# Two weight chunks per 256-token step, and a new order of the pieces, in a recurrence with two MLP layers

## The chip, the cores and the metric

One core of one Trainium2 chip runs the whole program. The metric is device time in microseconds; the median of three runs is compared.

## The reference

A gated linear recurrence over 768 time steps, for 4 batches and 8 heads of 48 channels, and then two MLP layers on all 3072 tokens, each 384 -> 2048 -> 384 wide:

```python
for t in range(S):
    state = alpha[:, :, t, :, None] * state + einsum('bhd,bhe->bhde', k[:, :, t], v[:, :, t])
    y[:, :, t] = einsum('bhd,bhde->bhe', q[:, :, t], state)
x = y.transpose(0, 2, 1, 3).reshape(3072, 384)
h = x @ w_in;   x = (h * tanh(softplus(h))) @ w_out      # layer 0
h = x @ w2_in;  out = (h * cos(h)) @ w2_out              # layer 1
```

The weights arrive as 64-bit floats.

## The kernel before

**Recurrence.** The 768 steps are cut into 12 chunks of 64; with two halves of the batch-heads (`hb`) that makes 24 units, in the list `order`. A unit loads decays (`ld_a`), keys, queries and values; two running products on VectorE (`scan`, L290, and `scan2`, L308) turn decays into factors; `keys` (L312) and `queries` (L322) multiply them in; TensorE does `turn` (L339), `scores` (L353, L354), `out_mm` (L370, L371) and `state_mm` (L431); `causal` (L360, L361) masks. The state is carried in the tiles `three` and scaled by GpSimd (`state_mul`, L450). `QPOOL` and `KPOOL` list the units whose `queries` and `keys` run on GpSimd instead of VectorE. The first eight units (`n < 8`) have start times of their own (`EARLY`); later ones are tied to MLP steps.

**Blocks and steps.** Tokens form 6 blocks of 512 (two chunks of 64 time steps x 4 batches), weights 16 chunks (`fc`) of 128 hidden channels. A step is one block and one weight chunk: nine matmuls into the PSUM tile `h` (`mm1`, L484 to L486), an elementwise chain, nine matmuls into three accumulators `acc` (`mm2`, L544 to L546). Both products are done with a high and a low part of each operand, three matmuls per product. In layer 0 the chain is sigmoid, arctan (`angle`, L492, L493) and sine (`sines`, L497) on ScalarE, a product (`gated`, L500) and the rounded high part (`act_c`, L524, a cast on VectorE; in layer 1 the cast is L526 on ScalarE), and the low part (`pool_c`, L531) on GpSimd. Sigmoid and arctan need one activation table, sine another, so sines are done for two steps at a time (`PAIR`, `pairs`). In layer 1 the chain is L505, L509, L512, L515, L518.

The first five chunks of block 0 run as half steps of 256 tokens (`HALVES`): all five on the first 256 tokens (`c0 = 0`), for which units 0 and 1 are enough, then all five on the second 256. `SHARED` makes two neighbouring blocks go through the same chunks one after the other: block 0 with chunks 0 to 7, block 1 with 0 to 7, then 8 to 15 for each.

**Weights.** A chunk is loaded (`ld_w`, L205) and converted: `conv_a` (L214, VectorE) moves low bits; the sign is taken either by `conv_a2` (L218, VectorE) or, for the chunks in `SIGNS`, by `conv_s` (L223, ScalarE); `conv_b` (L228, ScalarE) rescales, `conv_c` (L232, VectorE) joins, `conv_d` rounds the high part (L238 on ScalarE, or L236 on VectorE for chunks in `ROUNDS`), `conv_e` (L241, GpSimd) gives the low part. Layer 1's chunks are converted while layer 0 ends, in the tiles `three`. At most five raw chunks (tag `x`) are there at once.

**The order.** Every instruction is a piece with an engine, a cost, a due time, predecessors and buffers. `Plan.order` plays the pieces through once with these costs: whenever an engine is free it starts the ready piece with the smallest due time whose buffers are free. Instructions are emitted in that order, and each engine then runs its own instructions in it. All loads go through SyncE's queue. The due times are made of constants: `START`, `STEP`, `EARLY`, `CONV` (how long ahead of its first use a chunk is converted), `LOAD_K` and the like.

Of the kernel before, what the change touches and what calls it, by code (L numbers as in the profile page):

```python
# [13 lines left out]
F32 = mybir.dt.float32  # L14
# [22 lines left out]
START = [2.41] * 5 + [1.14] * 5 + [0.29] * 6  # L37
ATT = -0.89
# [4 lines left out]
BASE = (-1.08, 1.07, 2.87, 9)  # L43
LAG = 0.27
LOAD_K, LOAD_Q, LOAD_V, LOAD_W = 0.34, 0.74, 3.21, 9.99
LATE = -8.64
SPLIT = 7.29, 2.05
CONV = (5.15,) * 4 + (8.17,) * 4 + (30.0,) * 8
ELEM, SECOND, EVAC, FILLED = 7.7, 5.39, 5.39, -1.58
# [92 lines left out]
def chunked_path(ctx: ExitStack, tc: tile.TileContext, q, k, alpha, v1, ve, vo, w1, w2, const, out):  # L142
# [5 lines left out]
    def stile(shape, dtype, tag, name):  # L148
        return sb.tile(shape, dtype, tag=tag, bufs=BUFS[tag], name=name)
# [315 lines left out]
    for la, b, f0, f1 in phases:  # L465
        nh = HALVES.get((la, b), 0) if f0 == 0 else 0
        starts[len(steps)] = (la, b, f0)
        steps += [(la, b, fc, c, c + UT) for c in (0, UT) for fc in range(nh)] + [(la, b, fc, 0, N) for fc in range(max(nh, f0), f1)]
        ends[len(steps) - 1] = (la, b, f0)
        if f1 < NFC:  # L470
            split.add((la, b))
    phase_of = {}
# [4 lines left out]
    def mm1(i):  # L477
        la, b, fc, c0, c1 = steps[i]
        h = h_[i] = ps.tile([P, c1 - c0], F32, tag="h", bufs=3, name="h")
        hi, lo = wh[la, fc], wl[la, fc]  # L480
        for kc in range(3):
            f = slice(kc * P, kc * P + P)
            xh, xl = (x[:, kc, c0:c1] for x in xr[la, b])
            nc.tensor.matmul(h, hi[:, f], xh, start=kc == 0, stop=False)  # L484
            nc.tensor.matmul(h, hi[:, f], xl, start=False, stop=False)  # L485
            nc.tensor.matmul(h, lo[:, f], xh, start=False, stop=kc == 2)  # L486
# [3 lines left out]
    def angle(i):  # L490
        ta_[i] = stile([P, steps[i][4] - steps[i][3]], F32, "ta", "ta")
        nc.scalar.activation(ta_[i], h_[i], AF.Sigmoid, scale=-1.0)  # L492
        nc.scalar.activation(ta_[i], ta_[i], AF.Arctan)  # L493
# [26 lines left out]
    def act_c(i):  # L520
        la, b, fc, c0, c1 = steps[i]
        gh_[i] = stile([P, c1 - c0], F32R, "gh", "gh")
        if la == 0:
            nc.vector.tensor_copy(gh_[i], ta_[i])  # L524
        else:
            nc.scalar.copy(gh_[i], ta_[i])  # L526

    def pool_c(i):
        la, b, fc, c0, c1 = steps[i]
        gl_[i] = stile([P, c1 - c0], F32R, "gl", "gl")  # L530
        nc.gpsimd.tensor_tensor(gl_[i], ta_.pop(i), gh_[i].bitcast(F32)[:, :], op=ALU.subtract)  # L531

    def mm2(i):
        la, b, fc, c0, c1 = steps[i]
# [4 lines left out]
        hi, lo = wh[la, fc], wl[la, fc]  # L539
        gh, gl = gh_.pop(i), gl_.pop(i)  # L540
        first, last = i in starts, i in ends
        for d in range(3):
            f = slice(DM + d * P, DM + d * P + P)
            nc.tensor.matmul(acc[d][:, c0:c1], hi[:, f], gh, start=first, stop=False, skip_group_check=True)  # L544
            nc.tensor.matmul(acc[d][:, c0:c1], lo[:, f], gh, start=False, stop=False, skip_group_check=True)  # L545
            nc.tensor.matmul(acc[d][:, c0:c1], hi[:, f], gl, start=False, stop=last, skip_group_check=True)  # L546
# [30 lines left out]

    ticks = {}
# [14 lines left out]
    def dve(alone, beside):  # L593

        return lambda now: (beside if plan.free[POOL] > now + 0.3 * alone else alone, LAG)

    def dma(kib):
        return lambda now: (kib / 330.0, 2.0)

    due = [T0]  # L600
    for i, st in enumerate(steps):
        due.append(due[-1] + (STEP if st[4] - st[3] == N else HSTEP) + (START[i] if i < len(START) else ATT if st[0] == 0 and st[1] < NB - 1 else 0.0))
    n0 = sum(st[0] == 0 for st in steps)

    pairs, i = [], 0
    while i < n0:
        left = next(e for e in ends if e >= i) + 1 - i
        size = left % PAIR if i in starts and left % PAIR else PAIR
        pairs.append(list(range(i, i + size)))
        i += size  # L610
# [16 lines left out]
    for i, (la, b, fc, c0, c1) in enumerate(steps):  # L627
        half = c1 - c0 < N
        w = (lambda x: 0.5 * x + 0.05) if half else (lambda x: x)
# [25 lines left out]
        add(("act_c", i), DVE if la == 0 else ACT, dve(w(0.42), w(0.75)) if la == 0 else w(0.57), d + (6.2 if la == 0 else 7.3) - ELEM, functools.partial(act_c, i), [(prev, i), ("act_c", i - 1)], [("gh", ("gh", i))], [])  # L655
        add(("pool_c", i), POOL, w(1.4), d + 8 - ELEM, functools.partial(pool_c, i), [("act_c", i), ("pool_c", i - 1)], [("gl", ("gl", i))], [("ta", i)])
        add(("mm2", i), PE, pe(w(2.04)), d2, functools.partial(mm2, i), [("pool_c", i)] + ([("mm2", i - 1)] if i else []),
            [(f"acc{x}", ("acc", *phase_of[i], x)) for x in range(3)] if i in starts else [], [("gh", i), ("gl", i)] + [("w", la, fc), ("w2", la, fc)])
# [67 lines left out]
    index = {ph: i for i, ph in starts.items()}  # L726
    at_step = {2: index[0, 0, SHARED[0, 0]], 3: index[0, 2, 0] - 4, 4: index[0, 3, 0] - 8, 5: index[0, 4, 0] - 12}
    beside = {b: due[i] for b, i in at_step.items()}
    gate = {2: index[0, 1, 0] + 2, **{b: at_step[b] - 1 for b in range(3, NB)}}
    for n, s in enumerate(order):  # L730
# [20 lines left out]
        add(("keep_end", s), POOL, 0.6, d + 1, f(keep_end, s), [("scan", s)], [], [("Pt", n)])  # L751
# [224 lines left out]
```

## Time and profile before

| | |
|---|---|
| median of three runs | 958.46 us (958.07 to 958.48) |
| the profiled execution | 957.87 us, of which the span from first to last instruction is 956.1 us |
| TensorE busy | 908.7 us, 95% |
| ScalarE busy | 705.6 us, 74% |
| VectorE busy | 564.1 us, 59% |
| GpSimd busy | 471.0 us, 49% |
| mean granted TensorE clock | 0.988 |

Busy shares are means over stages that differ: the start, where TensorE lacks work, and long stretches in which it never stops. A table by stretch is of more use.

### The profile page before, as it was taken

How to read it: one execution, taken by the hardware profiler on the slowest of the kernel's cores; microseconds unless marked ns; L12 is line 12 of the kernel's file. 1: busy time of each engine (PE TensorE's matmuls, PEld its weight loads, DVE VectorE, ACT ScalarE, POOL GpSimd, SP SyncE). 2: the span in 40 equal slices, each digit the busy share in tenths (PEclk: the TensorE clock that was granted, in tenths of full speed). 3: DMA queues.
4: the chain of work that ended last, by engine and by line, in shares of the span. 5: the costliest groups of instructions: out<-in, count | busy, mean ns of one | idle time of the engine just before them, and what ended most of it. 6: DMA issues, size and time to landing. Idle time of an engine off the chain costs nothing.

```text
span 956.1 us, 15552 instructions
## 1 busy us (share of the span) xinstructions
PE 908.7 (95%) x5972; PEld 741.2 (78%) x5972; DVE 564.1 (59%) x757; ACT 705.6 (74%) x1077; POOL 471.0 (49%) x344
## 2 busy tenths in 40 slices
PE   5688889999999999999999999999999999999997
PEld 4577667788877787888887768788888888888886
DVE  7588999848847757612699697534443423333331
ACT  4999599777678688687999899866655666655653
POOL 4756748636336445343378567534423424332333
PEclk9979899999999999999999999999999999999999
DMA  8542543212313312120022222000000000000000
GB/s 252 172 131 90 171 129 110 68 34 75 92 44 99 91 44 85 38 72 1 27 80 93 70 95 99 2 1 1 34 34 1 1 33 1 34 1 1 34 0 36
DMA packets 25183, 59.09 MB, mean 62 GB/s; under 512 B 3856, under 2 KB 7568, under 8 KB 25104
## 3 DMA queue, kind: packets, MB, share of 16 engines
q1 hardware_dynamic: 25104, 58.05, 19.0%
q8 instruction: 47, 0.77, 0.3%
q14 instruction: 32, 0.26, 0.1%
HBM read 52.53 MB, written 4.72 MB: 60 GB/s over the span
## 4 chain that ended last, share of the span: by engine, by line
PE 71%; DVE 11%; ACT 8%; issue 4%; DMA 3%; POOL 2%; SPq 0%; POOLq 0%; DVEq 0%; ACTq 0%
PE acc L544 11%; PE h L484 11%; PE acc L546 11%; PE acc L545 11%; PE h L486 11%; PE h L485 11%; PE sc L353 2%; PE y L370 2%; DVE three L214 1%; DVE three L232 1%; PE dS L431 1%; DVE ta L500 1%; DVE three L218 1%; POOL three L322 1%; ACT three L223 1%
## 5 line engine op out<-in xcount | busy, mean ns | idle before, releaser
L531 POOL TENSOR_TENSOR gl<-ta,gh 128x512 fp32r<-128x512 f32 (+1 forms) x197 | 288.6, 1471 | 341.6 <-ACT gh L526 202.0
L484 PE MATMUL h<-xhi,wh 128*128 128x512 f32 (+1 forms) x591 | 234.0, 396 | 7.9 <-DVE ta L500 4.8
L544 PE MATMUL acc<-gh,wh 128*128 128x512 f32 (+1 forms) x591 | 232.0, 393 | 0.0
L546 PE MATMUL acc<-gl,wh 128*128 128x512 f32 (+1 forms) x591 | 228.5, 387 | 2.8 <-POOL gl L531 2.8
L486 PE MATMUL h<-xhi,wl 128*128 128x512 f32 (+1 forms) x591 | 229.0, 387 | 0.8 <-POOL wl L241 0.8
L485 PE MATMUL h<-xlo,wh 128*128 128x512 f32 (+1 forms) x591 | 229.2, 388 | 0.0
L545 PE MATMUL acc<-gh,wl 128*128 128x512 f32 (+1 forms) x591 | 227.4, 385 | 0.0
L512 DVE SCALAR_TENSOR_TENSOR tb<-tb,ta 128x512 f32<-128x512 f32 x96 | 80.5, 838 | 116.6 <-ACT tb L509 116.6
L484 PEld LDWEIGHTS h<-xhi,wh 128*128 128x128 f32 x591 | 112.6, 191 | 36.3 <-DVE ta L500 8.0
L546 PEld LDWEIGHTS acc<-gl,wh 128*128 128x128 f32 x591 | 111.4, 188 | 27.0 <-POOL gl L531 4.8
L486 PEld LDWEIGHTS h<-xhi,wl 128*128 128x128 f32 x591 | 112.9, 191 | 23.8 <-POOL wl L241 1.3
L544 PEld LDWEIGHTS acc<-gh,wh 128*128 128x128 f32 x591 | 111.2, 188 | 23.5 <-issue 0.6
L485 PEld LDWEIGHTS h<-xlo,wh 128*128 128x128 f32 x591 | 112.9, 191 | 21.0
L545 PEld LDWEIGHTS acc<-gh,wl 128*128 128x128 f32 x591 | 111.4, 188 | 21.1
L518 DVE TENSOR_TENSOR ta<-h,tb 128x512 f32<-128x512 f32 x96 | 66.4, 692 | 94.3 <-ACT tb L515 94.3
L500 DVE TENSOR_TENSOR ta<-h,ta 128x512 f32<-128x512 f32 (+1 forms) x101 | 65.5, 662 | 74.5 <-ACT ta L497 73.5
L505 ACT ACTIVATE ta<-h 128x512 f32<-128x512 f32 x96 | 57.4, 598 | 68.8 <-POOL gl L531 42.0
L526 ACT CAST gh<-ta 128x512 fp32r<-128x512 f32 x96 | 59.9, 624 | 48.3 <-PE acc L545 45.8
L492 ACT ACTIVATE ta<-h 128x512 f32<-128x512 f32 (+1 forms) x101 | 58.2, 577 | 35.7 <-PE h L486 33.8
L492 ACT ACT_TABLE_LOAD x50 | 64.2, 1283 | 25.6 <-PE h L486 24.7
L450 POOL TENSOR_TENSOR three<-three,aend 48x384 f32<-48x384 f32 x44 | 43.9, 997 | 47.7 <-DVE three L443 41.5
L497 ACT ACT_TABLE_LOAD x51 | 65.4, 1283 | 0.9
(119 smaller groups left out, 1262.9 us busy)
## 6 DMA issues: line engine op xcount, KB each, us to landing
wr<-in_w_dram SPq DMA_DIRECT2D x16, 768.0 KB, 5.4
three<-in_w_dram SPq DMA_DIRECT2D x16, 768.0 KB, 4.2
at<-in_alpha_chunks_dram SPq DMA_DIRECT2D x23, 227.9 KB, 2.8
qt<-in_q_chunks_dram SPq DMA_DIRECT2D x23, 224.0 KB, 3.2
kt<-in_k_chunks_dram SPq DMA_DIRECT2D x23, 224.0 KB, 2.7
vt<-in_v_chunks_dram SPq DMA_DIRECT2D x21, 192.0 KB, 2.5
out_dram<-o SPq DMA_DIRECT2D x15, 256.0 KB, 2.2
three<-in_ve_chunks_dram SPq DMA_DIRECT2D x24, 128.0 KB, 2.6
```

Source lines behind the costliest of these rows:

```text
L484: nc.tensor.matmul(h, hi[:, f], xh, start=kc == 0, stop=False)
L485: nc.tensor.matmul(h, hi[:, f], xl, start=False, stop=False)
L486: nc.tensor.matmul(h, lo[:, f], xh, start=False, stop=kc == 2)
L492: nc.scalar.activation(ta_[i], h_[i], AF.Sigmoid, scale=-1.0)
L497: nc.scalar.activation(ta_[i], ta_[i], AF.Sin, scale=-2.0, bias=quarter)
L500: nc.vector.tensor_tensor(ta_[i], h_.pop(i), ta_[i], op=ALU.mult)
L512: nc.vector.scalar_tensor_tensor(out=tb_[i], in0=tb_[i], scalar=MAGIC, in1=ta_[i], op0=ALU.subtract, op1=ALU.subtract)
L518: nc.vector.tensor_tensor(ta_[i], h_.pop(i), tb_.pop(i), op=ALU.mult)
L531: nc.gpsimd.tensor_tensor(gl_[i], ta_.pop(i), gh_[i].bitcast(F32)[:, :], op=ALU.subtract)
L544: nc.tensor.matmul(acc[d][:, c0:c1], hi[:, f], gh, start=first, stop=False, skip_group_check=True)
L545: nc.tensor.matmul(acc[d][:, c0:c1], lo[:, f], gh, start=False, stop=False, skip_group_check=True)
L546: nc.tensor.matmul(acc[d][:, c0:c1], hi[:, f], gl, start=False, stop=last, skip_group_check=True)
```

## The change

- `HALVES` goes from 5 to 6, and a half step now takes two chunks: `mm1` fills the two 256-wide halves of one 512-wide `h` with chunk `fc` and chunk `fc + 1`, the elementwise chain runs once over 512 columns, and `mm2` uses both. Block 0's first phase becomes 6 such steps and 2 whole ones (before: 10 half steps and 3 whole ones).
- `pairs` is built by runs of equal token range, with an odd first step in the first two phases.
- `SIGNS` falls from 16 chunks (layer 0: 0 to 7, layer 1: 8 to 15) to 11 (layer 0: 6, 7, 13; layer 1: 7 to 12, 14, 15). The rest take the VectorE path.
- `ROUNDS` grows from 8 chunks (layer 1: 0 to 7) to 17 (6 in layer 0, 11 in layer 1).
- `CASTS` says which steps' cast runs on ScalarE: 36 of 96 in layer 0 (before none), among them all 8 of the first phase; 38 of 96 in layer 1 (before all).
- `QPOOL` (before units 0 to 7) becomes 0, 3 to 7, 10 to 13, 16, 18, 19, 21, 22; `KPOOL` (before 5) becomes 5, 8, 14, 18, 19, 22, 23.
- `SHARED` for blocks 4 and 5 of layer 0 and 0 and 1 of layer 1 goes from 8 to 9 chunks.
- The constants of the due times and some piece costs change, with `CONV` now given per chunk for both layers; so pieces of all kinds come in another order. The program computes the same.

```diff
-START = [2.41] * 5 + [1.14] * 5 + [0.29] * 6
-T0, HSTEP = 25.52, 2.94
-HALVES = {(0, 0): 5}
-SHARED = {(0, 0): 8, (0, 4): 8, (1, 0): 8}
-EARLY = [0.0, 4.2, 7.83, 16.25] + [29.44 + 10.0 * n for n in range(4)]
+START = [4.15, 3.93, 4.03, -0.51, -0.08, 0.33, 1.06, 12.04, 20.83, 11.01]
+T0 = 25.5
+HALVES = {(0, 0): 6}
+SHARED = {(0, 0): 8, (0, 4): 9, (1, 0): 9}
+EARLY = [-0.37, 4.27, 7.5, 12.41, 29.45, 39.7, 50.82, 52.58]
-LOAD_K, LOAD_Q, LOAD_V, LOAD_W = 0.34, 0.74, 3.21, 9.99
+LOAD_K = -0.2
+LOAD_Q = 0.64
+LOAD_V = 2.68
+LOAD_W = -6.72
-CONV = (5.15,) * 4 + (8.17,) * 4 + (30.0,) * 8
+CONV = [-13.5, 10.98, 5.15, 5.15, 6.6, 5.75, 17.4, 17.74, 64.23, 59.89, 47.3, 46.69, 53.76, 39.38, 50.81, 57.96, 45.96, 44.85, 37.68, -9.62, 28.12, 11.06, -1.46, 45.99, 52.6, 47.2, 62.39, 45.76, 15.8, 39.55, 0.98, 15.49]
-QPOOL, KPOOL = range(8), (5,)
-SIGNS = {(0, fc) for fc in range(8)} | {(1, fc) for fc in range(8, NFC)}
-ROUNDS = {(1, fc) for fc in range(8)}
+QPOOL = {0, *range(3, 8), *range(10, 14), 16, *range(18, 20), *range(21, 23)}
+KPOOL = {5, 8, 14, *range(18, 20), *range(22, 24)}
+SIGNS = {*((0, fc) for fc in (6, 7, 13,)), *((1, fc) for fc in (7, 8, 9, 10, 11, 12, 14, 15,))}
+ROUNDS = {*((0, fc) for fc in (6, 8, 9, 10, 11, 13,)), *((1, fc) for fc in (1, 2, 4, 5, 6, 7, 9, 11, 12, 13, 15,))}
+CASTS = {*range(0, 8), 17, 21, 23, *range(30, 32), *range(34, 39), 42, 46, *range(49, 63), 90, 92, *range(96, 98), *range(99, 104), 119, *range(128, 145), 149, *range(151, 156), *range(168, 172), 178, 188, *range(191, 193), *range(194, 200)}
...
-        steps += [(la, b, fc, c, c + UT) for c in (0, UT) for fc in range(nh)] + [(la, b, fc, 0, N) for fc in range(max(nh, f0), f1)]
+        steps += [(la, b, (fc, fc + 1), c, c + UT) for c in (0, UT) for fc in range(0, nh, 2)] + [(la, b, (fc,), 0, N) for fc in range(max(nh, f0), f1)]
...
-        la, b, fc, c0, c1 = steps[i]
-        h = h_[i] = ps.tile([P, c1 - c0], F32, tag="h", bufs=3, name="h")
+        la, b, fcs, c0, c1 = steps[i]
+        h_[i] = ps.tile([P, N], F32, tag="h", bufs=3, name="h")
+        for j, fc in enumerate(fcs):
+            h = h_[i][:, j * UT : j * UT + c1 - c0]
...
-        if la == 0:
+        if i not in CASTS:
             nc.vector.tensor_copy(gh_[i], ta_[i])
         else:
             nc.scalar.copy(gh_[i], ta_[i])
...
+    runs = []
+    for i in range(n0):
+        if i == 0 or i in starts or steps[i][3:] != steps[i - 1][3:]:
+            runs.append([])
+        runs[-1].append(i)
+    pairs = []
+    for run in runs:
+        odd = 1 if run[0] < index[0, 0, SHARED[0, 0]] else len(run) % PAIR
+        pairs += ([run[:odd]] if odd else []) + [run[i : i + PAIR] for i in range(odd, len(run), PAIR)]
```

## Rows read from the trace of the kernel before

**Rows 1.** Busy us (and instructions) of each engine by stretch, granted clock, DMA.
```profile
0.00:25.00 25.00, 13.98 (x196) 11.73 (x196) 17.84 (x25) 10.80 (x17) 12.46 (x15) 1.00 0.88 255
25.00:75.00 50.00, 37.52 (x460) 32.97 (x458) 34.52 (x51) 47.30 (x75) 33.57 (x25) 0.90 0.45 143
75.00:125.00 50.00, 41.94 (x493) 33.99 (x494) 45.79 (x61) 36.41 (x55) 35.14 (x27) 0.93 0.48 151
125.00:175.00 50.00, 45.76 (x302) 35.47 (x301) 48.11 (x54) 47.21 (x68) 35.09 (x20) 0.97 0.27 87
...
200.00:470.00 270.00, 269.52 (x2201) 217.65 (x2201) 158.63 (x251) 209.42 (x311) 122.23 (x100) 1.00 0.19 57
470.00:545.00 75.00, 73.07 (x318) 58.75 (x317) 68.77 (x72) 67.54 (x86) 50.53 (x28) 1.00 0.25 85
545.00:605.00 60.00, 56.30 (x243) 44.73 (x242) 44.78 (x43) 55.31 (x81) 42.53 (x25) 1.00 0.22 79
605.00:950.00 345.00, 345.00 (x1522) 285.49 (x1521) 128.35 (x175) 212.83 (x363) 128.09 (x98) 1.00 0.03 12
```
The columns are: stretch, its length, then PE, PEld, DVE, ACT, POOL, and PEclk, DMA share, GB/s.

**Rows 2.** Chain that ended last, 0 to 50 us: start, us, what.
```profile
11.55 7.37 DMA qt<-in_q_chunks_dram
...
19.09 5.87 POOL three L322
...
27.74 1.91 ACT wr L223
...
30.32 1.82 ACT wr L223
...
35.42 4.50 POOL wl L241 x2
```

**Rows 3.** Timeline of VectorE, 29 us: start, us, what [idle before <-releaser].
```profile
29.68 0.96 DVE L232 SCALAR_TENSOR_TENSOR wr<-wr 128x768 uint32<-128x768 uint32 x1 [5.67 <-ACT wr L223]
```

**Rows 4.** Groups by line, whole run: busy us, mean ns | idle before.
```profile
L526 ACT CAST gh<-ta 128x512 fp32r<-128x512 f32 x96 | 59.9, 624 | 48.3 <-PE acc L545 45.8 <-POOL gl L531 1.5 <-DVE ta L518 0.6
...
L524 DVE CAST gh<-ta 128x512 fp32r<-128x512 f32 (+1 forms) x101 | 55.0, 562 | 0.6 <-issue 0.5
...
L322 DVE TENSOR_TENSOR three<-qt,Pt 112x512 f32<-112x512 f32 x16 | 17.2, 1077 | 7.2 <-PE y L371 3.4 <-DMA qt<-in_q_chunks_dram 2.8 <-PE y L370 0.9
...
L223 ACT ACTIVATE wr<-wr 128x768 f16<-128x768 f32 x8 | 15.5, 1933 | 0.1
...
L218 DVE TENSOR_SCALAR wr<-wr 128x768 uint16<-128x768 uint16 x8 | 12.9, 1617 | 0.1
...
L236 DVE CAST wh<-three 128x768 fp32r<-128x768 f32 x8 | 8.5, 1066 | 0.1
```

**Rows 5.** Timeline of SyncE's queue, 24 to 38 us.
```profile
24.97 0.33 SPq L270 DMA_DIRECT2D qt<-in_q_chunks_dram  x1
37.17 0.31 SPq L265 DMA_DIRECT2D kt<-in_k_chunks_dram  x1
```

**Rows 6.** Chain, pitch of one matmul: 256 columns at 68 us, 512 at 191 us.
```profile
68.05 0.12 PE h L486
...
191.10 0.23 PE h L485
```

**Rows 7.** Waits of TensorE: us in total, times, longest.
```profile
PE h L484 <- DVE ta L500: 4.8, 4, 2.9
```

**Rows 8.** Timeline of ScalarE, 40 to 42 us.
```profile
40.25 1.28 ACT L497 ACT_TABLE_LOAD   x1
41.55 0.51 ACT L497 ACTIVATE ta<-ta,quarter 128x256 f32<-128x256 f32 x1
```

**Rows 9.** Timeline of VectorE and GpSimd, 99 to 105 us.
```profile
99.91 2.00 POOL L531 TENSOR_TENSOR gl<-ta,gh 128x512 fp32r<-128x512 f32 x1
100.96 3.68 DVE L218 TENSOR_SCALAR wr<-wr 128x768 uint16<-128x768 uint16 x1
101.87 1.86 POOL L241 TENSOR_TENSOR wl<-wr,wh 128x768 fp32r<-128x768 f32 x1
```

More of the change, by code (lines that the diff above doesn't have):

```diff
@@ L471, in chunked_path @@
             split.add((la, b))
+    n0 = sum(st[0] == 0 for st in steps)
     phase_of = {}
@@ L477, in mm1 @@
     def mm1(i):
-        la, b, fc, c0, c1 = steps[i]
-        h = h_[i] = ps.tile([P, c1 - c0], F32, tag="h", bufs=3, name="h")
[L480 to L486, printed above, removed]
+        la, b, fcs, c0, c1 = steps[i]
+        h_[i] = ps.tile([P, N], F32, tag="h", bufs=3, name="h")
+        for j, fc in enumerate(fcs):
+            h = h_[i][:, j * UT : j * UT + c1 - c0]
+            hi, lo = wh[la, fc], wl[la, fc]
+            for kc in range(3):
+                f = slice(kc * P, kc * P + P)
+                xh, xl = (x[:, kc, c0:c1] for x in xr[la, b])
+                nc.tensor.matmul(h, hi[:, f], xh, start=kc == 0, stop=False)
+                nc.tensor.matmul(h, hi[:, f], xl, start=False, stop=False)
+                nc.tensor.matmul(h, lo[:, f], xh, start=False, stop=kc == 2)
     def angle(i):
-        ta_[i] = stile([P, steps[i][4] - steps[i][3]], F32, "ta", "ta")
+        ta_[i] = stile([P, N], F32, "ta", "ta")
         nc.scalar.activation(ta_[i], h_[i], AF.Sigmoid, scale=-1.0)
@@ L520, in act_c @@
     def act_c(i):
-        la, b, fc, c0, c1 = steps[i]
-        gh_[i] = stile([P, c1 - c0], F32R, "gh", "gh")
-        if la == 0:
+        gh_[i] = stile([P, N], F32R, "gh", "gh")
+        if i not in CASTS:
             nc.vector.tensor_copy(gh_[i], ta_[i])
@@ L538, in mm2 @@
         acc = acc_[ph]
[L539 to L546, printed above, removed]
+        gh2, gl2 = gh_.pop(i), gl_.pop(i)
+        for j, fc in enumerate(fcs):
+            hi, lo = wh[la, fc], wl[la, fc]
+            gh, gl = (g[:, j * UT : j * UT + c1 - c0] for g in (gh2, gl2))
+            first, last = i in starts and j == 0, i in ends
+            for d in range(3):
+                f = slice(DM + d * P, DM + d * P + P)
+                nc.tensor.matmul(acc[d][:, c0:c1], hi[:, f], gh, start=first, stop=False, skip_group_check=True)
+                nc.tensor.matmul(acc[d][:, c0:c1], lo[:, f], gh, start=False, stop=False, skip_group_check=True)
+                nc.tensor.matmul(acc[d][:, c0:c1], hi[:, f], gl, start=False, stop=last, skip_group_check=True)
     sums = {}
@@ L576, in chunked_path @@
     add = plan.add
+    index = {ph: i for i, ph in starts.items()}
     ticks = {}
@@ L597, in dma @@
     def dma(kib):
-        return lambda now: (kib / 330.0, 2.0)
+        return lambda now: (kib / 265.0 + (0.8 if now == 0.0 else 0.0), 2.0)
     due = [T0]
     for i, st in enumerate(steps):
[L602 to L610, printed above, removed]
+        due.append(due[-1] + STEP + (START[i] if i < len(START) else ATT if st[0] == 0 and st[1] < NB - 1 else 0.0))
+    runs = []
[7 more added lines that the diff above has]
+        pairs += ([run[:odd]] if odd else []) + [run[i : i + PAIR] for i in range(odd, len(run), PAIR)]
     pair_of = {i: k for k, pair in enumerate(pairs) for i in pair}
@@ L625, in chunked_path @@
     last = {st[:2]: i for i, st in enumerate(steps)}
-    for i, (la, b, fc, c0, c1) in enumerate(steps):
+    for i, (la, b, fcs, c0, c1) in enumerate(steps):
         half = c1 - c0 < N
-        w = (lambda x: 0.5 * x + 0.05) if half else (lambda x: x)
         d = due[i]
@@ L654, in chunked_path @@
                 prev = nm
[L655 to L658, printed above, removed]
+        add(("act_c", i), *((DVE, dve(0.42, 0.75)) if i not in CASTS else (ACT, 0.6)), d + (6.2 if la == 0 else 7.3) - ELEM, functools.partial(act_c, i), [(prev, i), ("act_c", i - 1)], [("gh", ("gh", i))], [])
+        add(("pool_c", i), POOL, 1.4, d + 8 - ELEM, functools.partial(pool_c, i), [("act_c", i), ("pool_c", i - 1)], [("gl", ("gl", i))], [("ta", i)])
+        add(("mm2", i), PE, pe(2.04), d2, functools.partial(mm2, i), [("pool_c", i)] + ([("mm2", i - 1)] if i else []),
+            [(f"acc{x}", ("acc", *phase_of[i], x)) for x in range(3)] if i in starts else [], [("gh", i), ("gl", i)] + [(w, la, fc) for fc in fcs for w in ("w", "w2")])
         if i in ends:
@@ L705, in chunked_path @@
         for fc in range(NFC):
-            i = next(i for i, st in enumerate(steps) if st[0] == la and st[2] == fc)
-            d = due[i] - (CONV[fc] if la == 0 else 45)
+            i = next(i for i, st in enumerate(steps) if st[0] == la and fc in st[2])
+            d = due[i] - (CONV[la * NFC + fc])
             f = functools.partial
```

36 lines of the change are left out of this document (19 added, 17 removed).

## The prediction

> **What bounds the kernel now.** I read the table by stretch first, since busy shares of the whole run hide the stages [rows 1]. From 200 to 470 us TensorE stands still for 0.48 us in all, from 605 to 950 for nothing: there an edit to another engine can cost but gain next to nothing. What TensorE lacks lies in three places. In the first 175 us it is idle for 11.0 + 12.5 + 8.1 + 4.2 = 35.8 us, and its granted clock falls to 0.90 to 0.97, part of the time therefore at the lower of its two levels, after the pauses. From 470 to 545 it is idle for 1.9 us, from 545 to 605 for 3.7 us. So about 41 us and some cold clock are all that an order of pieces can win back; what is won at the start passes through to the end, because the stretches behind it are full of TensorE work.
>
> The reader then asks the same table which engine is short in each part of the start. From 25 to 75 us it is ScalarE (47.3 of 50 busy) while VectorE has 15.5 us free. From 75 to 125 it is VectorE (45.8 of 50), from 125 to 175 VectorE (48.1) with ScalarE (47.2) close behind. The chain of waits [rows 2] names the pieces of the first 40 us: the queries of unit 2 wait for their load (7.37 us behind weights in the DMA queue), then take 5.87 us on GpSimd, then ScalarE makes two signs of 1.91 and 1.82 us in front of work that the first MLP step waits for, then GpSimd makes two low parts of weights. VectorE meanwhile waits 5.67 us in one place, for such a sign [rows 3].
>
> **Part by part.** The sum is made against the profiled execution, 957.87 us, whose span is 956.1; it lies 0.59 us under the median of the three runs.
>
> *Signs of chunks 0 to 5, and queries of units 1 and 2, to VectorE.* On the chain the signs take 1.91 + 1.82 = 3.73 us, and the queries 5.87, for which VectorE took 1.08 us on average elsewhere [rows 4]: 4.8 us less. Together up to 8.5. The cover for the new VectorE work is its own wait of 5.67 us [rows 3]: two signs at 1.62 [rows 4] and one set of queries at 1.08 make 4.3 us, which fit. Not all of the 8.5 can come through: behind it the chunk conversions, the state's scaling on GpSimd and the first step's inputs are next, and the first step now needs two finished chunks instead of one. If nothing but the signs came through it would be 3.7; if GpSimd's low parts now wait for the longer VectorE work, less. I take 5.0, between 2 and 8.5. Where the 5 us come from, the next unit is what is late: in SyncE's queue its keys go out 12.2 us after its queries, waiting for the scores of the unit before [rows 5], and with them the weight load queued behind. These shift with the scores. The due times put keys 0.84 us behind queries (0.64 + 0.20; before 0.40), so where keys go first it is because their buffer comes free first. A key load in front of the queries' holds them up, and the weights behind both, for as long as it waits itself; I take 0 (no order of the changed queue is in this trace), with 2 us lost as the bound, as a unit's queries have slack of most of the 12.2.
>
> *ScalarE from 25 to 75 us.* It loses three more signs there (chunks 3 to 5): 3 x 1.93 = 5.8 us of an engine without slack, while VectorE has 15.5 us free for 3 x 1.62 = 4.9. Ten half-step chains become six double ones, on all engines, which is also shorter. Against this come casts, 8 x 0.62 = 5.0 us, later than most of this stretch. I take 3.0 us of gain, between 0 (the state's chain, not ScalarE, sets the pace) and 5.8.
>
> *VectorE from 75 to 125 us.* The casts of the eight first steps leave it: I put what lies after 75 us at 8 x 0.56 = 4.5 us. The rounding of chunks 6 and 8 to 10 comes on it, 4 x 1.07 = 4.3 [rows 4]. That is level; double-width products save some instructions: 1.0 gain, between -3 and 3. *From 125 to 175*: the sign of chunk 13 (1.62) and the keys of unit 8 (a product of the queries' size, so about 1.08) leave VectorE, two roundings (2.1) come on it: 0.6 us less; I take 0.5, between -2 (GpSimd, at 35 of 50, gets these keys and slows the rest) and 2.
>
> *TensorE's own work.* A half-width matmul has a pitch of 0.12 us and a full one 0.23 [rows 6]. First phase before: 10 x 18 x 0.12 + 3 x 18 x 0.23 = 34.0 us; after: 12 x 18 x 0.12 + 2 x 18 x 0.23 = 34.2. A loss of 0.2.
>
> *Nine shared chunks, 470 to 545 us.* Two odd groups more for blocks 4 and 5 are four more table loads, 4 x 1.28 = 5.1 us, on a ScalarE with 7.5 us free of 75; TensorE has idled there for `gated` (4.8 us with the start's waits) [rows 1, 7]. I take 1.0 lost, between -1 and 3. On such loads a row and a rule differ: the sine begins 1.30 us after its table load does, so a switch costs 1.28 to 1.30 [rows 8]. The Trainium skill (ScalarE: Activation LUTs, "What ACT_TABLE_LOAD costs") adds a drain of 1.38 us to each, 2.66 us in all. By that rule the four would cost an estimated 10.6 us, and the term would be nearer its upper bound; the trace does not agree.
>
> *545 to 605 us.* Layer 1's casts, roundings and one sign move to VectorE: about 10 x 0.56 + 5 x 1.07 + 1.6 = 12.6 us on 44.8 of 60, so 57 of 60, while ScalarE falls from 55.3 by a like amount. The neck changes engine. I take 0, between 3.7 gained (all of TensorE's idle) and 6 lost.
>
> *Edits put at nothing.* Casts of full stretches, in both directions, queries and keys of the units from 10 on, and the later units' places (`BESIDE`): covered by TensorE. From 605 to 950 some 42 casts on VectorE make 24 us on an engine with 217 free; without cover they would cost up to these 24, which nothing in the row suggests. ScalarE from 200 to 470 has 61 us free for the casts it gets.
>
> Sum: -5.0 - 3.0 - 1.0 - 0.5 + 0.2 + 1.0 + 0 = -8.3. From 957.87 that is 949.6, and against the median 950.2.
>
> **The rivals.**
> *A. The start closes up further.* If the units, once freed of the long GpSimd queries and ScalarE signs, keep VectorE busy before 75 us as it is after, half of its 22.6 idle us of the first 75 is used: 11 us, plus the 5.8 of ScalarE's signs and up to 3 between 75 and 175, so about 20: 938.5. For it: VectorE is idle only there. Against: the load of unit 2's queries and the fixed first 11 us stay.
> *B. VectorE becomes the neck.* Through 175 us it gets six signs (9.7), six roundings (6.4) and two sets of queries (2.2), 18.3 us; it loses eight casts (4.5), one sign (1.6) and one unit's keys (1.1), some 7 us. That is 11 us more, and after 75 us the engine has 6 free. If the six signs come late instead of into the early gap, the end moves by what doesn't fit, 11 - 6 = 5 us, to 958.5 + 5 = 963.5. It decides from the point at which under 5 us of the new work land before 75 us. How it could get worse: a sign, 1.62 us on average, took 3.68 as GpSimd worked from 99.91 to 103.73 beside it, and ended 0.9 us behind GpSimd's instruction [rows 9]. By the Trainium skill (SBUF — State Buffer, "Who interferes with whom") VectorE and GpSimd share a port pair under an exclusive lock, and whichever starts second waits for the other's whole instruction. The trace agrees here; by that rule each moved VectorE instruction may carry up to one GpSimd instruction of 1.86 us, which speaks against the change.
> *C. The gain is waited away.* The recurrence has eight units in series for block 1's inputs; if their loads and buffers keep the pace of before, the first phase ends where it did and the earlier first step only lengthens later pauses: terms one and two vanish, -1 to +1 is left: 958.
>
> **How the numbers follow.** My forecast (3 to 14 us saved, 945 to 955.5) 0.50; A 0.22; C 0.10; B 0.18. The predicted time is 950.2. The range leaves out about 1 in 10 on each side: down to 935, half of A's cases or more inside, since the best of all bounds, -8.5 - 5.8 - 3 - 2 + 0.2 - 1 - 3.7 = -23.8, is 934.7; up to 963, which takes in C and the milder half of B. A difference under 0.2%, about 1.9 us, can't be told from none. Faster: 0.50 + 0.22 and a fifth of C, 0.74; same 0.08; slower 0.18. The likeliest case's own range is 945 to 955.5.
>
> **What would show it.** Right: queries of unit 2 on VectorE in about 1 us; no ScalarE sign before 60 us; the first `h` matmul at about 32 us instead of 37; TensorE idle under 30 us before 175; VectorE over 38 of 50 busy from 25 to 75. Wrong: signs (L218) before 75 us with a mean over 2.5 us, or low parts (L241) waiting for VectorE; the second 256 tokens' input (L396) no earlier; `gated` waits from 470 to 545 over 8 us; pauses of TensorE after 605.

## The result, and the profile after

The changed kernel takes 948.1 us (four runs, 946.33 to 950.85) against 958.47 us (958.07 to 959.09) for the kernel before on the same chip: ratio 0.9894, 95% interval 0.9869 to 0.9918, so 10 us less. The prediction was 950.2. The profiled execution took 948.23 us with a span of 946.3, 9.6 us under that of before; the forecast sum was 8.3. Sign and size came out; the places in which the time was won did not. That the sum came out all the same is luck (see the part on why).

The table by stretch of the changed kernel, with the columns of [rows 1]; its last stretch ends at 940:

```profile
0.00:25.00 25.00, 12.55 (x248) 10.66 (x248) 21.57 (x30) 11.63 (x22) 7.92 (x14) 1.00 0.92 267
25.00:75.00 50.00, 35.05 (x412) 30.45 (x414) 48.14 (x50) 31.70 (x50) 37.94 (x22) 0.69 0.50 162
75.00:125.00 50.00, 47.10 (x529) 40.28 (x525) 40.67 (x55) 42.16 (x62) 32.51 (x21) 0.97 0.36 116
125.00:175.00 50.00, 45.80 (x324) 35.72 (x323) 48.15 (x53) 47.04 (x65) 36.46 (x23) 0.93 0.31 100
470.00:545.00 75.00, 73.71 (x325) 60.52 (x324) 59.52 (x66) 72.74 (x92) 45.55 (x28) 1.00 0.22 74
545.00:605.00 60.00, 59.47 (x262) 48.75 (x262) 53.00 (x57) 49.26 (x73) 39.58 (x24) 1.00 0.23 80
605.00:940.00 335.00, 334.85 (x1478) 276.95 (x1477) 148.14 (x225) 180.22 (x302) 138.32 (x98) 1.00 0.04 15
```

Read against [rows 1]: from 0 to 175 us TensorE is idle for 12.5 + 15.0 + 2.9 + 4.2 = 34.5 us, where it was 35.8. In this execution the idle time only moved from 75–125 (8.1 before) into the first 75 us. VectorE, with 15.5 us free from 25 to 75 before, is now full there (48.1 of 50), and ScalarE fell from 47.3 to 31.7. From 470 to 605 TensorE issues 325 + 262 = 587 matmuls where it issued 318 + 243 = 561. At full width, 26 matmuls are 5.9 us.

Since TensorE has hardly a gap elsewhere, progress can be read as a count: the matmuls of the MLP (`h` and `acc`, those of 256 columns counted as half) that have begun at a fixed time. By 470 us, when all work of the recurrence on TensorE is done, it is 1394 after and 1376 before; by 800 us 2836 and 2792. A matmul takes 0.227 us at full pitch (288 between two evacuations of accumulators, 767.61 and 832.89 us). So the lead is 18 x 0.227 = 4.1 us at 470 and 44 x 0.227 = 10.0 at 800. None of these matmuls is missing from the two traces (3564 records after, 3546 before, as many as the steps make); how far the counts scatter from one execution to the next is told behind the experiments. **The start gave 4.1 us and the middle 5.9**; the forecast was 9.3 (terms one to five) and -1.0.

**The start.** The chain of waits of the changed kernel, 0 to 50 us (start, us, what), with lines that answer to [rows 2]; line numbers are those of the changed kernel (`queries` is L331, `scan` L299, `conv_a` L223, the sign on VectorE L227, `conv_c` L241, the low part L250, the input's low part `y_lo` L405):

```profile
8.68 6.12 DMA wr<-in_w_dram
...
15.88 0.07 DVE three L331
...
25.31 1.85 POOL wl L250
...
29.16 1.90 POOL spare L331
...
32.62 0.15 ACT st L385
32.77 0.04 issue
32.81 1.51 PE y L391 x12
34.35 0.49 ACT xhi L399
34.86 0.56 DVE xlo L405
```

The load of unit 2's queries (7.37 us), its product on GpSimd (5.87) and the two signs on ScalarE are gone from the chain. The product took 0.66 us on VectorE, begun at 15.74. But unit 3's queries on GpSimd (29.16) are on the chain in their place: in ScalarE's queue the copy that they lead to stands ahead of a copy for unit 2 (`st`, 32.62), and TensorE waited 3.8 us for this one, before twelve matmuls (L391) that stand in its order ahead of the first MLP step; between the two stand the score matmuls of unit 3 (L362, L363), from 34.23 on. The first 256 tokens' input was ready at 32.07 + 0.53 = 32.6 us, but the first `h` matmul began at 36.13 (37.07 before). It could not have begun with both chunks at 32.6 either, for GpSimd made the second chunk's low part only then, behind unit 3's state:

```profile
31.01 3.83 POOL L459 TENSOR_TENSOR three<-three,aend 48x384 f32<-48x384 f32 x2
34.92 1.85 POOL L250 TENSOR_TENSOR wl<-wr,wh 128x768 fp32r<-128x768 f32 x1
```

The recurrence does run ahead, and then loses it again. Starts of two pieces of each unit in the two timelines of VectorE (us):

| unit | 0 | 1 | 2 | 3 | 4 | 5 | 6 | 7 |
|---|---|---|---|---|---|---|---|---|
| `scan`, before | 3.84 | 8.27 | 16.90 | 35.03 | 50.13 | 65.89 | 77.84 | 91.40 |
| `scan`, after | 3.91 | 8.23 | 13.39 | 26.45 | 39.01 | 56.63 | 72.00 | 94.62 |
| `y_lo`, before | 30.56 | 34.54 | 48.22 | 61.66 | 75.34 | 88.26 | 105.99 | 117.89 |
| `y_lo`, after | 21.91 | 32.07 | 34.86 | 49.69 | 74.17 | 89.47 | 105.43 | 114.95 |

Unit 4 begins 11.1 us earlier and ends 1.2 us earlier. Where its lead went stands in VectorE's timeline (start, us, line, what):

```profile
49.69 0.54 DVE L405 TENSOR_TENSOR xlo<-y,xhi 128x384 fp32r<-128x384 f32 x1
50.33 1.98 DVE L241 SCALAR_TENSOR_TENSOR wr<-wr 128x768 uint32<-128x768 uint32 x1
52.23 2.11 DVE L223 TENSOR_SCALAR wr<-wr 128x768 uint16<-128x768 uint16 x1
54.38 2.45 DVE L227 TENSOR_SCALAR wr<-wr 128x768 uint16<-128x768 uint16 x1
56.63 1.20 DVE L299 TENSOR_TENSOR_SCAN Pt<-at,seg_start 112x520 f32<-112x520 f32 x1
57.75 1.47 DVE L452 TENSOR_TENSOR three<-three,dS 48x192 f32<-48x192 f32 x4
...
62.07 0.69 DVE L369 TENSOR_TENSOR three<-sc,cst 64x512 f32<-64x512 f32 x1
62.80 0.68 DVE L370 TENSOR_TENSOR three<-sc,cst 64x512 f32<-64x512 f32 x1
```

Three conversions of weights and unit 5's scan, 7.4 us, stand ahead of the state's addition (L452), for which TensorE waits before it turns unit 4's keys; its mask (L369, L370) follows at 62. Behind that, GpSimd holds unit 4 and unit 5 (same columns, first GpSimd, then ScalarE):

```profile
63.45 4.54 POOL L250 TENSOR_TENSOR wl<-wr,wh 128x768 fp32r<-128x768 f32 x1 [2.23 <-DMA kt<-in_k_chunks_dram]
67.95 1.52 POOL L321 TENSOR_TENSOR kt<-kt,at 112x512 f32<-112x512 f32 x1
69.43 1.17 POOL L331 TENSOR_TENSOR three<-qt,Pt 112x512 f32<-112x512 f32 x1
```

```profile
70.63 0.62 ACT L335 COPY three<-three 48x512 f32<-48x512 f32 x1 [2.15 <-POOL three L331]
71.27 0.60 ACT L504 ACTIVATE ta<-h 128x512 f32<-128x512 f32 x1
71.90 0.63 ACT L505 ACTIVATE ta<-ta 128x512 f32<-128x512 f32 x1
72.44 0.46 ACT L399 CAST xhi<-y 128x384 fp32r<-128x384 f32 x1
```

A low part of 4.54 us stands ahead of unit 5's keys and queries, ScalarE waits for these queries, and unit 4's input (`xhi`, L399) stands behind them there. What those conversions probably bought comes in the next stretch: by 75 us seven chunks have their low part where it was five, and from 75 to 125 TensorE lacks 2.9 us of work, not 8.1. That the one causes the other no run shows by itself. The groups of low parts from 25 to 75 us, after and before (count, busy us, mean ns, idle time before):

```profile
L250 POOL TENSOR_TENSOR wl<-wr,wh 128x768 fp32r<-128x768 f32 x7 | 17.4, 2483 | 6.5 <-issue 4.2 <-DMA kt<-in_k_chunks_dram 2.2
...
L241 POOL TENSOR_TENSOR wl<-wr,wh 128x768 fp32r<-128x768 f32 x5 | 10.1, 2021 | 2.5 <-ACT wh L238 2.5
```

**The middle.** TensorE's waits from 470 to 605 us (us in total, times, longest), all that are left; they answer to [rows 7]:

```profile
PE h L496 <- DVE ta L512: 1.3, 1, 1.3
PE h L496 <- DVE ta L530: 0.5, 1, 0.5
```

In the trace of before the same window has three groups: `gated` (L500), layer 1's product (L518) and a low part (L531).

```profile
PE h L484 <- DVE ta L518: 3.1, 2, 1.6
PE h L484 <- DVE ta L500: 1.9, 3, 0.8
PE acc L546 <- POOL gl L531: 0.6, 1, 0.6
```

TensorE's idle time was 5.6 us and is 1.8. The other 2 us of the 5.9 lie in busy time (561 x 0.227 = 127.2 of 129.4 busy us before, 133.1 of 133.2 after), and they belong to the same stops, which the idle time shows too short: measured from start to start, the first matmul behind a stop comes about 0.17 us later than the idle time says, and the one behind it another 0.11. Counted so, before has eleven stops that cost 8.5 us, and after has two that cost 2.4. Ten of the eleven, and both of the two, wait for VectorE's product (`gated` or layer 1's). So the gain of the middle is that this product now comes in time.

### The profile page after: what moved, and what is told of

It reads as the page before. It is cut to its first block, busy times and chain, and to the rows that moved or that the text cites. A ratio compares the mean times of both kernels' runs of the same rounds, so it can differ in the third digit from the quotient of the medians.

```text
span 946.3 us, 15561 instructions
## 1 busy us (share of the span) xinstructions
PE 904.3 (96%) x5990; PEld 742.1 (78%) x5990; DVE 573.2 (61%) x770; ACT 682.5 (72%) x1030; POOL 478.2 (51%) x352
## 4 chain that ended last, share of the span: by engine, by line
PE 80%; DVE 8%; ACT 5%; issue 4%; POOL 2%; DMA 1%; SPq 0%; POOLq 0%; ACTq 0%; DVEq 0%
PE h L496 13%; PE acc L556 12%; PE h L498 12%; PE h L497 12%; PE acc L558 12%; PE acc L557 12%; PE y L379 2%; PE sc L362 2%; PE dS L440 1%; DVE wr L241 1%; DVE wr L223 1%; POOL gl L541 1%; DVE Pt L299 1%; PE pt L348 1%; DVE tb L524 1%
## 5 line engine op out<-in xcount | busy, mean ns | idle before, releaser
L541 POOL TENSOR_TENSOR gl<-ta,gh 128x512 fp32r<-128x512 f32 x192 | 280.7, 1465 | 325.7 <-DVE gh L535 192.0
L517 ACT ACTIVATE ta<-h 128x512 f32<-128x512 f32 x96 | 57.6, 600 | 80.5 <-PE h L498 76.3
L535 DVE CAST gh<-ta 128x512 fp32r<-128x512 f32 x118 | 71.8, 613 | 61.7 <-PE acc L557 60.4
L512 DVE TENSOR_TENSOR ta<-h,ta 128x512 f32<-128x512 f32 x96 | 64.3, 684 | 62.8 <-ACT ta L509 62.3
L527 ACT ACTIVATE tb<-tb 128x512 f32<-128x512 f32 x96 | 60.6, 631 | 55.9 <-DVE tb L524 55.9
L504 ACT ACTIVATE ta<-h 128x512 f32<-128x512 f32 x96 | 57.6, 600 | 29.4 <-PE h L498 27.3
```

## The experiments

The change is many edits, and a plan makes one order of them. Twelve kernels undo parts of it, or do parts alone. All times are medians, ratios are to the kernel before in the same batch (958.67 us for runs e, 958.71 for f1 to f5, 959.13 for g and f6). The changed kernel itself was timed in the first batch alone, so the other runs are set against it by these ratios (its own is 0.9894, 0.9869 to 0.9918). Some edits change constants, from which the plan makes a new order; "order kept" means that the changed kernel's order stands and only an engine is swapped.

**e1_signs0.** Changed kernel, layer 0's signs as before (chunks 0 to 7 on ScalarE, chunk 13 on VectorE), order made anew.
```diff
-SIGNS = {*((0, fc) for fc in (6, 7, 13,)), ...
+SIGNS = {*((0, fc) for fc in range(8)), ...
```


> The changed kernel with the signs of layer 0's chunks 0 to 7 on ScalarE again (the plan is made anew with them). Theory S (the start's gain comes from signs leaving ScalarE, as the prediction had it): about 3 to 8 us slower than the changed kernel's 948.1, so 951 to 956, TensorE's first h matmul later. Theory D (the moved signs only filled VectorE, which is now 48 of 50 busy from 25 to 75 us, and bring nothing): 946 to 950.

947.6 us, 0.9888 (0.9869 to 0.9908): no loss at all. Its table by stretch:

```profile
25.00:75.00 50.00, 37.66 (x498) 34.20 (x495) 42.26 (x49) 44.35 (x59) 37.62 (x25) 0.78 0.53 168
75.00:125.00 50.00, 44.63 (x475) 37.43 (x474) 35.76 (x49) 35.16 (x53) 25.97 (x20) 0.90 0.36 113
```

ScalarE carries the signs (44.4 of 50) and VectorE has 8 us free. TensorE is busy 2.6 us more from 25 to 75, which is within what executions of one order differ by there (33.9 to 37.7), and 2.5 less from 75 to 125. With an order made for it, layer 0's signs can be on either engine; theory D holds.

**e3_layer1.** Changed kernel, layer 1's casts, roundings and signs as before, order made anew.
```diff
+SIGNS = {..., *((1, fc) for fc in range(8, NFC))}
+ROUNDS = {..., *((1, fc) for fc in range(8))}
+CASTS = {..., 90, 92, *range(96, 200)}
```


> The changed kernel with layer 1's casts all on ScalarE, layer 1's rounding on VectorE for chunks 0 to 7 and its signs on ScalarE for 8 to 15, as before. Theory L (levelling VectorE and ScalarE in layer 1 is what took TensorE's idle time from 5.6 to 1.8 us between 470 and 605 us): 3 to 6 us slower, 951 to 954, idle time back between 545 and 605. Prediction (that term is 0): 947 to 949.

952.99 us, 0.9938 (0.9919 to 0.9957): 4.9 us of the gain are gone. From 470 to 605 it issues 317 + 246 = 563 matmuls, two more than before, and 2.7 us of idle time are back between 545 and 605:

```profile
470.00:545.00 75.00, 72.85 (x317) 59.01 (x316) 68.14 (x67) 66.48 (x86) 47.70 (x29) 1.00 0.23 74
545.00:605.00 60.00, 57.26 (x246) 46.92 (x245) 42.91 (x44) 51.64 (x76) 36.76 (x23) 0.97 0.23 80
```

**e4_shared8.** Changed kernel, blocks 4 and 5, and 0 and 1 of layer 1, share 8 chunks again.
```diff
-SHARED = {(0, 0): 8, (0, 4): 9, (1, 0): 9}
+SHARED = {(0, 0): 8, (0, 4): 8, (1, 0): 8}
```


> The changed kernel with 8 shared chunks again for blocks 4 and 5 of layer 0 and 0 and 1 of layer 1. If the ninth shared chunk is what gained between 470 and 605 us: 2 to 5 us slower, 950 to 953. If it only costs its four table loads, as the prediction had it: 1 us faster, 947.

952.63 us, 0.9947 (0.9924 to 0.9970), its runs from 949.43 to 955.55. Taking out the ninth chunk, which I had put at a loss of 1.0, costs 4.5 us by the median. The profiled execution, the fastest of the five, lost only 1.3, with 574 matmuls from 470 to 605 where the changed kernel has 587, so the size is uncertain.

**e5_conv45.** Changed kernel, layer 1's chunks all converted 45 us ahead, as before.
```diff
-d = due[i] - (CONV[la * NFC + fc])
+d = due[i] - (CONV[fc] if la == 0 else 45)
```


> The changed kernel with layer 1's conversions all due 45 us ahead of their first use again, instead of a time for each chunk. If spreading the conversions gained between 470 and 605 us: 2 to 5 us slower, 950 to 953. If not: 947 to 949.

949.07 us, 0.9904 (0.9886 to 0.9921): about 1 us, not clear of the scatter.

**f1_q12pool, f2_casts0, f6_q3dve.** Changed kernel, order kept. f1: queries of units 1 and 2 on GpSimd again. f2: the casts of the first eight steps on VectorE again. f6: unit 3's queries, which are on the chain, on VectorE too.
```diff
+... nc.gpsimd if qe == POOL or n in (1, 2) else nc.vector ...
+        if i not in CASTS or i < 8:
+... nc.gpsimd if qe == POOL and n != 3 else nc.vector ...
```


> The changed kernel, every engine's order kept, with the queries of units 1 and 2 multiplied on GpSimd again. Theory Q (they held up the start, as the prediction had it): 2 to 5 us slower than the changed kernel's 948.1, 950 to 953. Rival (they are waited away by the units that follow): 947 to 949.

> The changed kernel, every engine's order kept, with the casts of the first phase's eight steps on VectorE instead of ScalarE. If VectorE is the neck of the start and these casts' leaving it is what gained: 8 x 0.56 = up to 4.5 us slower, 950 to 952.5. If the start is set by the chain of units: 947 to 949.

> The changed kernel, order kept, with the queries of unit 3 on VectorE too. In the changed kernel they run on GpSimd from 29.12 to 31.05 us, and ScalarE waits behind them before it copies what the first MLP step needs. If that holds up the start: first h matmul 1 to 2 us earlier than 36.1, and 946 to 947.5. If the later units wait the gain away, or VectorE, 48 of 50 busy there, is the neck: 947.5 to 949.5.

948.96 (0.9902, 0.9886 to 0.9919), 948.67 (0.9898, 0.9882 to 0.9915) and 948.13 us (0.9886, 0.9870 to 0.9903). None differs from the changed kernel by more than its scatter. f6 was meant to be the better version and isn't: its first `h` matmul began at 37.93 us, not 1 to 2 us before 36.13. With unit 3's queries on it, VectorE came later to that unit's keys (L321, ended at 35.88 and not at 33.32), and TensorE's score matmuls, ahead of the first MLP step, waited for those:

```profile
PE sc L362 <- DVE kt L321: 2.0, 1, 2.0
```

**f5_pairs.** Kernel before, with the two-chunk steps alone: its old engines and times, only the steps' form and the constants that belong to it (`START` and `HALVES` as below; `HSTEP` goes).
```diff
-START = [2.41] * 5 + [1.14] * 5 + [0.29] * 6
-HALVES = {(0, 0): 5}
+START = [4.5] * 5 + [2.0] * 3 + [0.29] * 3
+HALVES = {(0, 0): 6}
```


> The kernel before with nothing but the two-chunk steps: half steps take two chunks (6 instead of 5 chunks per half, the same total of due times up to the second phase, the odd first steps), all else as before. If the double steps are the start's gain: 3 to 6 us faster than before, 952.5 to 955.5. If they only do the same work in other portions, or wait for two chunks: 957 to 963.

963.21 us, 1.0052 (1.0035 to 1.0069): slower than before by 4.5 us; the lead at 470 us is -4.8. With these due times (the old total, spread anew) the new form of the steps costs; with others it was not run.

**f4_before_l1.** Kernel before with the change's engines for layer 1 (signs, roundings, casts), order made anew.
```diff
+SIGNS = {*((0, fc) for fc in range(8)), *((1, fc) for fc in (7, 8, 9, 10, 11, 12, 14, 15))}
+ROUNDS = {(1, fc) for fc in (1, 2, 4, 5, 6, 7, 9, 11, 12, 13, 15)}
+LAYER1 = {*range(96, 98), *range(99, 104), 119, ..., 178, 188, 191}
...
+    return la == 0 or i - 5 not in LAYER1
```


> The kernel before with nothing but layer 1's engine choices of the changed kernel: which casts, roundings and signs run on VectorE and ScalarE. Theory L (they alone level the two engines between 470 and 605 us): 4 to 6 us faster than before, 952.5 to 954.5. If they only pay with the new order: 957 to 959.5, or slower, as VectorE was at 69 of 75 from 470 to 545.

957.71 us, 0.9990 (0.9980 to 0.9999): 1 us. What costs 4.9 us when it is taken out is worth 1 when it is put in alone.

**g2_before_mid.** f4, and nine shared chunks, and the change's conversion times of layer 1: all three parts of the middle in the kernel before.
```diff
+SHARED = {(0, 0): 8, (0, 4): 9, (1, 0): 9}
+d = due[i] - (CONV[fc] if la == 0 else (45.96, 44.85, 37.68, -9.62, 28.12, ...)[fc])
```


> The kernel before with all of the changed kernel's parts for the stretch from 470 to 605 us: nine shared chunks, layer 1's engine choices, layer 1's conversion times. Theory M (these parts together gain 4 to 6 us there, and each needs the others): 952.5 to 955. Rival (without the new order of the start they bring no more than the engine choices alone, which gave 0.1%): 957 to 959.

956.85 us, 0.9976 (0.9967 to 0.9986): 2.3 us, of 5.9, which is in neither range. Its table by stretch:

```profile
470.00:545.00 75.00, 75.00 (x333) 62.10 (x332) 49.62 (x61) 69.67 (x91) 42.33 (x27) 1.00 0.15 53
...
605.00:938.00 333.00, 331.08 (x1460) 273.49 (x1459) 161.15 (x234) 185.80 (x309) 141.66 (x98) 1.00 0.06 19
```

TensorE is without a gap from 470 to 545, where it has 15 matmuls more than before, and pays 1.9 us back in gaps after 605, where before had none.

**g3_after_oldmid.** Changed kernel without those three parts: e3, e4 and e5 together (e3's lines left out here).
```diff
+SHARED = {(0, 0): 8, (0, 4): 8, (1, 0): 8}
...
+            d = due[i] - (CONV[fc] if la == 0 else 45)
```


> The changed kernel with the old parts for that stretch: eight shared chunks, layer 1's engine choices and its conversion times as before. Theory M: 4 to 6 us slower than 948.1, so 952 to 954.5; what is left against before, 4 to 6 us, is the start. If the undone parts add up (5 and 4.5 and 1 us slower each by itself): 957 to 959.

949.46 us, 0.9908 (0.9887 to 0.9928): 1.4 us lost, which is within the scatter and in neither range, where e3 and e4 alone each lost more than 4. From 470 to 605 it issues 321 + 258 = 579 matmuls, 18 more than before, without any of the three parts:

```profile
470.00:545.00 75.00, 73.08 (x321) 59.86 (x320) 63.74 (x68) 67.77 (x89) 52.29 (x29) 1.00 0.26 85
545.00:605.00 60.00, 58.75 (x258) 47.83 (x257) 44.27 (x47) 57.42 (x84) 41.26 (x25) 1.00 0.25 80
```

**g1x_engines.** Changed kernel, order kept, and every choice of engine as before (signs, roundings, casts, queries, keys). What is left of the change is the order, the double steps and the nine shared chunks.
```diff
+        return fc < 8 if la == 0 else fc >= 8
...
+        if la == 1 and fc < 8:
...
+        if i < 96:
...
+... nc.gpsimd if n == 5 else nc.vector ...
+... nc.gpsimd if n < 8 else nc.vector ...
```
The lines are, in turn, the choice of engine for signs, roundings, casts, keys and queries.

> The changed kernel's order of pieces, double steps and nine shared chunks, but every engine choice as before: signs, roundings, casts, queries and keys each run where the kernel before ran them, at the place in the program that the changed kernel gives them. Theory O (the order is what gains at the start, and the engine choices pay between 470 and 605 us only): 950 to 954, with TensorE as far along at 211 us as in the changed kernel. Rival (the engine choices carry the start too): 955 to 962.

951.64 us, 0.9932 (0.9914 to 0.9949): 7.5 of the 10 us come without any of the engine choices, and almost all of it in the middle:

```profile
470.00:545.00 75.00, 73.88 (x325) 60.59 (x324) 67.07 (x71) 68.39 (x88) 49.02 (x28) 1.00 0.22 74
545.00:605.00 60.00, 60.00 (x266) 49.54 (x266) 45.14 (x49) 54.30 (x81) 39.06 (x23) 1.00 0.23 79
```

That is 591 matmuls where the changed kernel has 587, with layer 1's old engines. At 470 us it leads by 0.5 us only. The time lies in theory O's range, but its places are the wrong way round: at 211 us it has begun 448 MLP matmuls where the changed kernel has 462, and the middle gains without the engine choices.

The count of matmuls for all kernels, as us ahead of the kernel before (0.227 us each):

```
                 by 470 us   470 to 800   together   median against before
changed             4.1         5.9         10.0        -10.4
e1_signs0           3.6         6.1          9.7        -11.1
f1_q12pool          2.9         6.1          9.1         -9.8
f2_casts0           5.0         5.9         10.9        -10.0
f6_q3dve            1.6         5.9          7.5        -11.0
e5_conv45           4.5         5.0          9.5         -9.6
g3_after_oldmid     4.5         4.5          9.1         -9.7
e4_shared8          5.4         3.2          8.6         -6.0
e3_layer1           2.3         1.1          3.4         -5.7
g1x_engines         0.5         7.0          7.5         -7.5
g2_before_mid      -0.7         3.2          2.5         -2.3
f4_before_l1        0.2         0.7          0.9         -1.0
f5_pairs           -4.8        -0.7         -5.4         +4.5
```

The first three columns are of one profiled execution each. How far the start scatters can be read from kernels that differ only later: up to 409 us e3, e4, e5 and g3 have the changed kernel's order on every engine and in the load queue, and f4 and g2 have that of the kernel before.

| | order of before (3 traces) | order of after (5 traces) |
|---|---|---|
| first `h` matmul, us | 36.55 to 37.07 | 35.66 to 37.84 |
| TensorE idle, 0 to 175 us | 35.4 to 37.6 | 29.6 to 36.0 |
| TensorE idle, 75 to 125 us | 7.3 to 8.1 | 2.7 to 3.7 |
| granted clock, 25 to 75 us | 0.76 to 0.90 | 0.69 to 0.80 |
| lead at 470 us | -0.7 to 0.2 | 2.3 to 5.4 |

Part of the scatter is there from the first loads on: unit 0's input (`y_lo`) is begun at 21.9 us in the changed kernel's trace and at 23.6 in e3's, where VectorE waited 0.84, 0.46 and 0.80 us for loads of keys, decays and weights (0.21 for weights in the changed kernel's), and e3 stays about 1.7 us behind from there to unit 5. So the start's gain is shown, 4.2 us on average, but nothing under 3 us is read from the first column. The middle scatters less: f1, f2 and f6, which keep the changed kernel's order, have 5.9 to 6.1. The four runs of the changed kernel spread over 4.5 us, those of before over 1.0 in that batch and 2.2 to 4.7 in the others.

## Why the prediction was right, and where it was not

The forecast had the start gain 9.3 us and the middle lose 1.0. The start gave 4.1 and the middle gained 5.9: the first is 5.2 too large, the second 6.9 too small, and the sum, 8.3 against 9.6, came out because the two errors nearly cancel. That is luck.

**Signs and queries to VectorE (-5.0) and ScalarE from 25 to 75 (-3.0)** were too large together: the whole start gave 4.1, and what each of the two gave can't be separated. Of the five signs of being right three came: queries in 0.66 us, no sign on ScalarE before 60.73 us, VectorE at 48.1 of 50. Two didn't: the first `h` matmul came at 36.13, not 32, and TensorE was idle for 34.5 us before 175, not under 30.

The step that failed is that the freed 8.5 us of the chain would reach the MLP step. Over the five traces of the new order the first `h` matmul begins at 36.7 us on average, over the three of the old order at 36.8: nothing of it came through. I had named what was next (conversions, the state's scaling, two finished chunks instead of one) and taken 5.0 all the same. In TensorE's order unit 2's copy and unit 3's scores stood in front, the copy stood on ScalarE behind unit 3's queries, and the second chunk's low part came at 34.92. Taking one of these away wasn't enough: with unit 3's queries on VectorE (f6) the scores waited for VectorE instead. Nor are the signs on ScalarE what held the start: with them back (e1) the kernel is as fast.

**VectorE from 75 to 125 (-1.0)** was too small: 5.2 us of idle time go there, and 4.4 on the average of the traces of each order. I costed that stretch by VectorE's load; two more chunks were ready at 75, which is the likely cause. **125 to 175** (-0.5): TensorE's idle time is the same 4.2.

Where in the start the 4.1 us lie isn't separated: the idle time up to 175 us scatters by more than that. g1x says what they hang on: with the same order and the old engines the lead is 0.5, outside the 2.3 to 5.4 of the five traces, and about 3.6 us of time are lost, so the engines are worth about that much inside this order. No single engine edit undone shows it (e1, f1, f2), and the new steps alone, with the due times of f5, cost 4.5 us. Order and engines do it together; which of the engine choices, beyond those tried, is open, and so is what the new times of the loads and of the first eight units bring, which no run changes alone.

**Nine shared chunks (+1.0) and 545 to 605 (0)** are the terms that failed in sign and size: together 5.9 us gained. Two steps failed: that the added table loads, on a ScalarE with little time free, would hold up `gated`, and that from 545 to 605 TensorE's waits would stay as they were (those for layer 1's product fell from 3.1 to 0.5 us). The four more table loads did cost ScalarE their 1.28 us each (the load, then the sine 1.29 us after the load's start, close to [rows 8]); here one of them, of an odd group:

```profile
486.03 1.28 ACT L509 ACT_TABLE_LOAD   x1
487.32 0.72 ACT L509 ACTIVATE ta<-ta,quarter 128x512 f32<-128x512 f32 x1
```

ScalarE is at 72.7 of 75 from 470 to 545, yet TensorE's waits for `gated` fell from 1.9 to 1.3 us: with the order that was there, these loads were hidden. My bound of 3.7 for the second term was all of TensorE's idle time from 545 to 605; it took no account of what a stop costs beyond its idle time, 2 us in the whole middle.

What makes the middle is the order. g1x has it with all the old engines (7.0 us), g3 has most of it with the old chunks, engines and conversion times (4.5 us), and the three parts bring 2.3 us in the order of before (g2). For e3 the cause of its loss is shown too: g1x has the same engines in layer 1 and keeps the gain, with the order left as it was, so what e3 lost it lost by the order that the plan made anew. That e4's loss has the same cause is argued, not shown, and g3, whose order was made anew as well, lost little. Which of the other due times (`ELEM`, `SECOND`, `EVAC`, `STEP`) carries the order of the middle was not run and stays open.

**Edits put at nothing** were nothing where I could see them: after 605 VectorE makes 52 casts (28.1 us) and TensorE lacks 0.15 us.

**The rivals.** A (the start closes further) fell: VectorE is as full early as it says, 21.6 + 48.1 us of 75, but the start gave 4. B (VectorE becomes the neck) fell by its own tests: the signs before 75 us take 1.47 us on average, not over 2.5, and VectorE has 69.7 - 52.4 = 17.3 us more work before 75 us, so the new work did land early. Its mechanism is there all the same, as conversions of 1.98 to 2.45 us ahead of unit 4's state, and in f6. C, that the gain is waited away, is what happened at the first MLP step and to the recurrence from unit 4 to unit 7, but not to the first phase: its accumulators are evacuated from 113.09 us on, not from 123.87.

## What to carry to other kernels

Where one plan orders all work, judge its constants as a bundle: a part taken out of a fitted plan shows a loss that the part doesn't bring when put in alone (4.9 against 1.0 us here). To separate order from engines, keep the order and swap the engines. Find where time was won by counting the bound engine's instructions at fixed times in both traces, since idle time alone missed a third of the middle's gain; measure first how far the same order scatters, with kernels that differ only later; and before a gain is claimed for an engine freed at the start, list what the first step still needs on every other queue.

## What was unexpected of the hardware

The granted TensorE clock from 25 to 75 us differs between executions of one order, from 0.76 to 0.90 in the old and from 0.69 to 0.80 in the new, so the fall from 0.90 in [rows 1] to 0.69 is at most in part the change's. Behind a pause the lower of its two levels can be seen in the changed kernel's trace, as matmuls of 256 columns 0.21 us apart, where [rows 6] have 0.12 (start, us, what); from 65.8 to 67.4 the granted clock is 0.50:

```profile
66.03 0.41 PE L498 MATMUL h<-xhi,wl 128*128 128x256 f32 x1
66.24 0.41 PE L496 MATMUL h<-xhi,wh 128*128 128x256 f32 x1
```

What this costs in all isn't separated here.

VectorE and GpSimd slow each other in single rows by more than the means that I used. The sign on VectorE took 1.01 us at 17.46, and 2.45 at 54.38 beside GpSimd's low part:

```profile
17.46 1.01 DVE L227 TENSOR_SCALAR wr<-wr 128x768 uint16<-128x768 uint16 x1
...
53.42 2.50 POOL L250 TENSOR_TENSOR wl<-wr,wh 128x768 fp32r<-128x768 f32 x1
```

By the Trainium skill (SBUF — State Buffer, "Who interferes with whom") the second to start of two instructions that need the shared port pair waits for the other's whole instruction; the trace agrees: this sign ended 0.91 us after the low part did, about its length alone. The lines of [rows 9] show that it can be more than one: there the sign began at 100.96 us, GpSimd's next instruction began at 101.87 and still went first, and the sign ended 0.91 us behind that one. So the prediction's "up to one GpSimd instruction" for each moved instruction was too low for its own row. Low parts average 2.48 us from 25 to 75, with VectorE full, where they averaged 2.02, but most of that is one of 4.54; the other six average 2.14.
